# A new order table for a gated linear attention kernel: other turns on every engine, other engines for some operations, 82 fill-in matmuls

## The chip, the cores and the metric

The kernel runs on one core of a Trainium2 chip. The core has five engines that run side by side, each through its own list in order: TensorE (PE, matmuls, with PEld for the weight loads), VectorE (DVE), ScalarE (ACT), GpSimd (POOL) and SyncE (SP, which here only issues DMAs). The metric is the device time of one execution in microseconds (us). The kernel before took 194.0, 195.34 and 195.01 us in three runs, a median of 195.01 us.

## What is computed

Inputs q, k, v, a_re, a_im have the shape (4 batches, 8 heads, 768 steps, 48). Per batch and head a complex state S of 48 x 48 is decayed by a at each step, k v^T is added, and q reads its real part:

```
mag   = sqrt(a_re^2 + a_im^2);  a = (a_re, a_im) * min(mag, 0.999) / (mag + 1e-6)
S_re, S_im = a_re*S_re - a_im*S_im + k v^T,  a_re*S_im + a_im*S_re
y[t]  = q[t] . S_re
x     = y with the heads side by side             # (4, 768, 384)
xn    = (x - mean(x)) / sqrt(var(x) + 1e-6) * g_ln
out   = x + relu(xn @ w_ch1) @ w_ch2              # 384 -> 1536 -> 384
```

## The kernel before

The 768 steps of a batch are cut into six chunks of 128. Two chunks are a pair, so there are twelve pairs (0 to 11), three to a batch, and 24 chunks. Pair P holds chunks 2P and 2P+1. Pair 0 alone does its gate work in two halves of four heads (`.0` and `.1` at the end of a name), so that its first results come earlier.

The recurrence is turned into matmuls. A decay is a magnitude and an angle, and both are summed over the steps of a chunk. For a pair the operations, by the names that the order table uses, are:

- loads on SP: `are`, `aim` (L440), `k`, `q`, `vf` (L399);
- gates: `ln` (L443, ACT) and `iv` (L445, ACT) of a_re, `r` = aim/are, `r2` its square, `u` = ln(1 + r2) (L457, ACT), `l` and `lc`, the log magnitude and its cap (L461, L464, DVE), `th`, the arctan (L480, ACT);
- sums over the steps on PE: `dec` of the log magnitudes (L472) and `ph` of the angles (L487, L491), which takes the last angle of the pair before from `car` (L501 or L504);
- `e` and `en`, exp of plus and minus the sum (L476, ACT), `sin` (L509) and `cos` (L520, or by `abs`, L526 or L528, and L532), with `qt` (L516, PE), which adds a quarter turn for pairs 0 to 3;
- products on DVE or GpSimd (all on line 289, a helper): `ke` = k en, `qe` = q e, and the stacks `ks`, `qs`, each product times cos (`.0`) and times sin (`.1`). `r` and `r2` have the same helper line. `pad` clears the stacks' unused columns;
- the stacks turned round, `ksT`, `qsT`: either by PE (`kT`, `qT`, L588) with a copy by DVE or ACT, or by a transposing DMA from SP (L593);
- `am`, the scores (L611), `atm`, the scores under the causal mask (DVE), `v` in bf16 (L407 or L409), `gm` and `G`, the state carried from chunk to chunk (L635, L639), with the decay from `dps` (L568) and `decc`; `y` (L661, L664), `x` a copy of it;
- the layer norm's sums `bn` (L674, L675) and `rstd` (L698 or L701), and the feed forward: `xtr` and `xT` turn x round (L682), `mm1` is x by w1 in three groups of two parts (L715), `relu` (L726 ACT, L728 DVE), `mm2` by w2 (L736), `ot` the output (L750 on DVE; or `oa` on ACT, L741, and `ot` on GpSimd, L748), `st` its store (L756).

The norm is folded into w1: `wp` and `wc` (L379, L383) change the weights in place, once at the start, after `wl.0` has loaded them (L359, from GpSimd's queue). `wl.1` (L361) loads w2. `tab` (L770) loads ACT's table, one for logarithm and exp, the other for arctan and sine; an ACT operation needs its table to be the one loaded last. `warm` is a fill-in matmul (L765): it multiplies constants into a bank that nobody reads, and needs only the constant `ue`.

What sets the order is one list written out by hand, `PLAN`. A token such as `qs.1.0.0:V` gives an operation, its engine (P, A, V, G, S) and, after P or for an operation that reads PSUM, the bank. `@name` adds a wait for another operation on top of the waits that the data ask for. Each engine runs its tokens in the order of the list, and an operation that must wait holds all that stands behind it on its engine. Operands live in rings of tiles (`RINGS`: three for `q`, two for `vf`, two for `xT` and `h`, and so on), so an operation also waits until the tile's former use is over; and PSUM has eight banks, which are handed from one user to the next in the order of the list.

```
for op in steps:
    if op.behind:
        tc.add_manual_dep(made[op.name][0], made[op.behind][-1].name, info,
                          reason="turns at the shared port")
```

Of the kernel before, what the change touches and what calls it, by code (L numbers as in the profile page):

```python
# [39 lines left out]
ue:G are.1.0:S are.0.0:S are.0.1:S aim.0.0:S pad.ks.1:G warm.0:P0 warm.1:P0 aim.0.1:S warm.2:P0 zdec:G  # L40
pad.qs.1:G warm.3:P0 warm.4:P0 aim.1.0:S pad.ks.0:G warm.5:P0 warm.6:P0 warm.7:P0 one:G cmean:G warm.8:P0
tab.log.0:A ln.1.0:A pad.qs.0:G warm.9:P0 warm.10:P0 aim.2.0:S qrow:G warm.11:P0 ln.0.0:A warm.12:P0 car0.1:G
warm.13:P0 warm.14:P0 iv.0.0:A car0.0:G warm.15:P0 warm.16:P0 pad.qs.2:G k.0.1:S ln.0.1:A warm.17:P0
warm.18:P0 pick:G warm.19:P0 iv.0.1:A r.0.0:V warm.20:P0 q.1.0:S iv.1.0:A warm.21:P0 warm.22:P0 r2.0.0:V
warm.23:P0 r.0.1:V warm.24:P0 u.0.0:A warm.25:P0 q.0.1:S warm.26:P0 r2.0.1:V warm.27:P0 uth:V u.0.1:A
warm.28:P0 r.1.0:V warm.29:P0 gln:S warm.30:P0 warm.31:P0 warm.32:P0 r2.1.0:V warm.33:P0 warm.34:P0 are.2.0:S
warm.35:P0 warm.36:P0 l.0.0:V warm.37:P0 warm.38:P0 tab.trig.1:A th.0.1:A warm.39:P1 lc.0.0:V th.1.0:A
ph.0.1:P0 k.0.0:S dec.0.0:P1 th.0.0:A car.0.1:V0 l.0.1:V sin.0.1:A0 q.0.0:S ph.0.0:P2 warm.40:P3 warm.41:P3
car.0.0:V2 q.1.1:S wgc:V ph.1.0:P4 lc.0.1:V tab.log.2:A u.1.0:A k.1.1:S wl.0:G@lc.0.1 dec.0.1:P3 car.1.0:V4
qt.0.1:P0 ln.2.0:A vf.0.0:S l.1.0:V warm.42:P6 ident:G warm.43:P6 warm.44:P6 warm.45:P6 e.0.0:A1 warm.46:P6  # L50
warm.47:P6 vf.0.1:S iv.2.0:A warm.48:P6 lc.1.0:V dec.1.0:P6 en.0.1:A3 r.2.0:V k.1.0:S en.0.0:A1 e.1.0:A6
are.3.0:S r2.2.0:V e.0.1:A3 qe.1.0.0:V u.2.0:A dps.0:P1 ke.0.0.0:V qe.0.0.0:V warm.49:P3 warm.50:P3 l.2.0:V
warm.51:P3 warm.52:P3 warm.53:P3 warm.54:P3 warm.55:P3 warm.56:P3 qe.0.1.0:V warm.57:P3 warm.58:P3
tab.trig.3:A sin.0.0:A2 ke.0.1.0:V cos.0.1:A0 qt.0.0:P2 lc.2.0:V sin.1.0:A4 warm.59:P3 qs.0.0.1:V warm.60:P3
ks.0.0.1:V cos.0.0:A2 ks.0.1.0:V qt.1.0:P4 qs.0.1.1:V th.2.0:A ks.0.1.1:V dps.1:P0 ks.0.0.0:V cos.1.0:A4
kT.1:P2 decc.1:V0 qs.0.1.0:V kT.0:P0 qs.0.0.0:V ksT.1:V2 qT.0:P3 qe.1.0.1:G@qs.0.0.0 qT.1:P4 qsT.0:V3 mask:G
aim.3.0:S tab.log.4:A en.1.0:A6 wp.0:P5 decc.0:V1 qs.1.0.1:V qsT.1:A4 dec.2.0:P2 qs.1.0.0:V vf.1.1:S wc.0.0:V5
ke.1.0.1:G@qs.1.0.0 ksT.0:A0 am.1:P6 wc.0.1:V5 qT.3:P4 vf.1.0:S ke.1.0.0:G e.2.0:A2 wc.0.2:V5 am.0:P0
en.2.0:A2 v.0:G q.2.1:S qsT.3:V4 ks.1.0.0:V ln.3.0:A gm.0:P2 q.2.0:S ph.2.0:P4 atm.1:V6 ks.1.0.1:G@ks.1.0.0
G.0:A2 iv.3.0:A k.2.0:S gm.1:P2 qT.2:P3 atm.0:V0 y.1:P6 r.3.0:G k.2.1:S kT.3:P7 G.1:V2 wp.1:P0 qsT.2:V3  # L60
tab.trig.5:A sin.2.0:A4 are.4.0:S y.0:P1 kT.2:P2 ksT.3:V7 x.0:A1 v.1:G qt.2.0:P4 th.3.0:A ksT.2:V2 xtr.0:P7
aim.4.0:S wl.1:G gm.2:P1 wc.1.0:V0 x.1:A6 ph.3.0:P2 G.2:A1 wc.1.1:V0 qe.2.0.0:G cos.2.0:A4 xtr.1:P6 wc.1.2:V0
gm.3:P1 xT.0:A7 qe.2.0.1:G am.3:P4 sin.3.0:A2 xT.1:V6 wp.2:P0 atm.3:V4 qs.2.0.0:G car.3.0:A2 am.2:P6 qt.3.0:P2
atm.2:V6 mm1.0.0.0:P4 cos.3.0:A2 qs.2.0.1:G mm1.0.0.1:P4 G.3:V1 y.3:P2 wc.2.2:V0 relu.0.0:A4 y.2:P1 x.3:V2
# [10 lines left out]
ot.1:V2 mm2.3.1:P1 iv.6.0:A bn.2:V mm1.2.0.1:P4 st.0:S bn.4:V rstd.1:G mm1.2.0.0:P4 st.1:S qs.3.0.1:V
mm1.2.1.1:P6 qs.3.0.0:V tab.trig.7:A th.5.0:A mm2.3.2:P1 ks.3.0.1:V relu.2.0:A4 ot.2:V0 mm1.2.1.0:P6 l.5.0:V
st.2:S qT.6:P2 th.4.0:A vf.3.1:S qT.7:P0 q.4.0:S qe.4.0.1:G@l.5.0 qsT.6:A2 kT.7:P3 qsT.7:V0 are.8.0:S
ph.4.0:P4 ke.4.0.0:G ksT.7:V3 relu.2.1:A6 are.7.0:S ot.3:V1 kT.6:P0 sin.4.0:A4 mm1.2.2.0:P2 r.6.0:V abs.4.0:A4
am.7:P6 vf.4.1:S ksT.6:V0 ke.4.0.1:G@r.6.0 mm1.2.2.1:P2 car.4.0:A4 atm.7:V6 cos.4.0:A am.6:P0 k.5.0:S
# [24 lines left out]
relu.5.2:V0 ph.9.0:P4 x.12:A3 y.13:P3 ot.9:V6 sin.9.0:A4 mm2.10.0:P0 qs.7.0.1:V x.13:A3 mm2.11.1:P2 abs.9.0:V4
car.9.0:A4 qsT.15:S xtr.13:P1 xtr.12:P3 ks.7.0.1:V mm2.10.1:P0 xT.12:V3 ksT.15:S mm2.10.2:P0 v.7:V
# [696 lines left out]
```

## Time and profile before

| | |
|---|---|
| three runs, us | 194.0, 195.34, 195.01 |
| span of the profiled execution, us | 193.1 |
| time of the profiled execution beside its span | not given on the page; the median of the runs is 1.9 above the span |
| busy: PE, DVE, ACT, POOL | 91%, 79%, 83%, 54% |
| first `mm1` matmul (L715) starts at, us | 39.79 |
| last matmul ends at about, us | 188.3 |
| granted PE clock | full, but for 24.0 to 27.4 (0.50) and the end |
| DMA | 37.04 MB, 192 GB/s over the span |

A row of the timeline gives the start and the length in us, the engine, the line, the operation, `out<-in` by the program's tile names without buffer numbers, shapes and a count; in brackets stands the engine's idle time before it and what ended it. A group's row gives the busy time, the mean in ns of one, the idle time before. The busy time of PE is modelled: matmuls are pipelined and their lengths overlap. Several operations share one helper line, so products are told apart by their tiles (`r`, written by `r`, `r2` and `u` alike, holds three of them).

### The profile page before, as it was taken

The page shows a single profiled execution, that of the slowest core. Times are in us where ns is not written, and L with a number is a line of the kernel's source. Part 1 is how long each engine was busy: PE and PEld are TensorE (multiplying, and loading weights), DVE is VectorE, ACT ScalarE, POOL GpSimd, SP SyncE. Part 2 cuts the span into 40 slices and gives each one's busy share as a digit, 9 for nine tenths or more (in the row PEclk, how much of TensorE's full clock was granted, in tenths as well). Part 3 has the DMA queues.
Part 4 walks back from the last instruction along what each step waited for, and adds up shares of the span by engine and source line. Part 5 has one row for each costly group of instructions (what it writes and reads, how often), then busy time and mean ns, then how long its engine had stood idle before and what let it go on. Part 6 is the DMA issues. An engine that isn't in the chain of part 4 may idle for free.

```text
span 193.1 us, 5126 instructions
## 1 busy us (share of the span) xinstructions
PE 175.3 (91%) x2042; PEld 133.6 (69%) x2042; DVE 151.7 (79%) x276; ACT 159.4 (83%) x222; POOL 104.8 (54%) x123
## 2 busy tenths in 40 slices
PE   5856597999999999999999989999989897999991
PEld 3643386689876877877867856868658676776860
DVE  0578979999779999799988978997987695657422
ACT  3899989979999999999989898888999856463460
POOL 8403038998334435489595950544857715593110
PEclk9999969999999999999999999999999999999998
DMA  5999999999999699979999997999997999997132
GB/s 159 275 215 185 201 207 239 213 188 220 210 201 214 195 260 231 220 152 226 188 233 168 212 220 106 195 235 205 230 196 150 140 203 147 252 127 203 44 122 83
DMA packets 129992, 37.04 MB, mean 192 GB/s; under 512 B 124976, under 2 KB 129584, under 8 KB 129968
## 3 DMA queue, kind: packets, MB, share of 16 engines
q1 hardware_dynamic: 128016, 34.35, 85.7%
q0 software_dynamic: 1952, 2.36, 7.4%
q8 instruction: 16, 0.26, 0.6%
q14 instruction: 8, 0.07, 0.1%
HBM read 28.31 MB, written 4.72 MB: 171 GB/s over the span
## 4 chain that ended last, share of the span: by engine, by line
PE 52%; DVE 17%; ACT 12%; DMA 7%; SPq 4%; issue 4%; POOL 2%; DVEq 0%; ACTq 0%
PE banks L736 16%; PE banks L715 15%; PE banks L588 5%; PE banks L611 3%; DMA qsT<-qs 3%; DMA aim<-in_a_im_dram 2%; SPq L593 2%; PE banks L491 2%; ACT L770 2%; DVE l L461 2%; DMA k<-in_k_dram 2%; ACT trig L509 2%; ACT th L480 2%; PE banks L661 2%; PE banks L682 2%
## 5 line engine op out<-in xcount | busy, mean ns | idle before, releaser
L736 PE MATMUL banks<-w2b,h 128*128 128x384 bf16 x288 | 54.5, 326 | 0.7 <-ACT trig L509 0.6
L715 PE MATMUL banks<-xT,w1b 128*128 128x256 bf16 x432 | 51.3, 273 | 0.0
L715 PEld LDWEIGHTS <-w1b 128*128 128x128 bf16 x432 | 41.3, 98 | 6.3 <-DVE xT L286 0.4
L736 PEld LDWEIGHTS <-h 128*128 128x128 bf16 x288 | 26.1, 97 | 14.6 <-issue 1.1
L289 DVE TENSOR_TENSOR atm<-banks,mask 128x1024 bf16<-128x1024 f32 x24 | 28.9, 1219 | 7.4 <-PE banks L611 7.2
L726 ACT ACTIVATE h<-banks 128x1024 bf16<-128x1024 f32 x26 | 26.3, 1020 | 5.4 <-PE banks L715 5.2
L289 POOL TENSOR_TENSOR qe<-q,e 128x384 bf16<-128x384 f32 x18 | 16.4, 917 | 22.8 <-DVE qs L289 8.4
L289 POOL TENSOR_TENSOR qs<-qe,trig 128x768 bf16<-128x768 bf16 x12 | 19.6, 1641 | 7.7 <-DVE ks L289 5.5
L770 ACT ACT_TABLE_LOAD x17 | 21.8, 1283 | 1.1 <-PEq L786 0.8
L289 POOL TENSOR_TENSOR ke<-k,en 128x384 bf16<-128x384 f32 x16 | 14.5, 916 | 9.9 <-DVE l L464 5.6
L289 POOL TENSOR_TENSOR ks<-ke,trig 128x768 bf16<-128x768 bf16 x9 | 14.7, 1642 | 7.7 <-DVE ks L289 6.8
L611 PE MATMUL banks<-qsT,ksT 128*128 128x128 bf16 x192 | 14.6, 219 | 1.7 <-DMA qsT<-qs 1.7
L728 DVE TENSOR_SCALAR h<-banks 128x1024 bf16<-128x1024 f32 x10 | 12.1, 1214 | 4.9 <-PE banks L715 4.9
L748 POOL TENSOR_TENSOR ot<-ot,x 128x384 f32<-128x384 f32 x8 | 7.2, 914 | 15.8 <-ACT ot L741 15.8
L611 PEld LDWEIGHTS <-ksT 128*128 128x128 bf16 x192 | 12.0, 97 | 4.0 <-issue 2.6
L491 PE MATMUL banks<-th,u_th 128*128 128x384 f16 (+1 forms) x52 | 11.9, 313 | 2.5 <-ACT th L480 2.5
L750 DVE SCALAR_TENSOR_TENSOR ot<-banks,rstd,x 128x384 f32<-128x384 f32 x16 | 9.8, 612 | 5.4 <-PE banks L736 3.5
L461 DVE SCALAR_TENSOR_TENSOR l<-r,w 128x768 f16<-128x768 f16 (+1 forms) x13 | 12.0, 926 | 2.0 <-ACT r L457 1.8
L674 DVE BATCH_NORM_STATS2 stats<-x 128x6 f32<-128x384 bf16 x24 | 13.1, 546 | 0.0
L289 POOL TENSOR_TENSOR r<-aim,are 128x768 f16<-128x768 f32 x6 | 10.9, 1817 | 4.1 <-ACT are L445 4.1
L443 ACT ACTIVATE w<-are 128x768 f32<-128x768 f32 (+1 forms) x13 | 10.3, 797 | 2.5 <-DMA are<-in_a_re_dram 2.5
L457 ACT ACTIVATE r<-r,one_b 128x768 f16<-128x768 f16 (+1 forms) x13 | 11.5, 887 | 0.7 <-DVE r L289 0.6
(95 smaller groups left out, 372.6 us busy)
## 6 DMA issues: line engine op xcount, KB each, us to landing
k<-in_k_dram SPq DMA_DIRECT2D x24, 192.0 KB, 4.1
q<-in_q_dram SPq DMA_DIRECT2D x24, 192.0 KB, 4.1
vf<-in_v_dram SPq DMA_DIRECT2D x24, 192.0 KB, 4.1
out_dram<-ot SPq DMA_DIRECT2D x24, 192.0 KB, 3.1
are<-in_a_re_dram SPq DMA_DIRECT2D x11, 384.0 KB, 4.5
aim<-in_a_im_dram SPq DMA_DIRECT2D x11, 384.0 KB, 4.9
w1b<-in_moe_w_ch_dram POOLq DMA_DIRECT2D x1, 1152.0 KB, 11.1
w2b<-in_moe_w_ch_dram POOLq DMA_DIRECT2D x1, 1152.0 KB, 12.5
```

Source lines behind the costliest of these rows:

```text
L289: {"DVE": nc.vector, "POOL": nc.gpsimd}[eng(name)].tensor_tensor(**kw)
L443: add(f"ln.{X}", lambda S_=S_: act(out=S_("w"), in_=S_("are"), func=AF.Ln), needs=[f"are.{X}"], uses=[("are", P), ("w", P)])
L457: add(f"u.{X}", lambda S_=S_: act(out=S_("r2"), in_=S_("r2"), func=AF.Ln, bias=one_b), needs=[f"r2.{X}", "one"], uses=[("r2", P)])
L461: nc.vector.scalar_tensor_tensor(out=S_("l"), in0=S_("r2"), scalar=0.5, in1=S_("w"), op0=ALU.mult, op1=ALU.add)
L491: nc.tensor.matmul(heads(ps[:, c]), lhsT=u_th[:, c, j], rhs=step(T("th", P), j), start=False, stop=(j == R - 1), skip_group_check=True)
L611: nc.tensor.matmul(ps[:, h], lhsT=T("ksT", n)[:, h], rhs=T("qsT", n)[:, h], start=True, stop=True)
L674: nc.vector.bn_stats(out=T("stats", n), in_=T("x", n))
L715: nc.tensor.matmul(ps[:, jj], lhsT=w1b[:, dc, ts(gi * JG + jj, C)], rhs=T("xT", P)[:, dc].rearrange("p c t -> p (c t)"), start=(dc == 0), ...
L726: act(out=dst, in_=src, func=AF.Relu)
L728: nc.vector.tensor_scalar(out=dst, in0=src, scalar1=0.0, scalar2=None, op0=ALU.max)
L736: nc.tensor.matmul(bank(f"o.{n}")[:, 0:DM], lhsT=T("h", P)[:, j, ts(c, C)], rhs=w2b[:, j], start=(j == 0), stop=(j == NJ - 1))
L770: g.add(f"tab.{nm}.{i}", lambda tab=tab: nc.scalar.preload_act_table_set(tab))
```

## The change

The order table is replaced as a whole; below it only the number of fill-in operations changes. Against the table before:

- the loads of pair 0's a_re stand ahead of pair 1's, and other loads have other turns: q of pair 0 comes behind a_im of pair 2 and k of pair 1, for example;
- on ACT the second half's `u` of pair 0 stands behind `th` and a change of tables; `sin` and `cos` of pairs 0 and 1 stand in one stretch; on DVE `car.0.0` stands ahead of `l.0.0`;
- 23 manual waits become 40. Most hold a GpSimd operation until a DVE one is over; `wl.0` waits for `ke.0.0.0`, `wl.1` for `gm.2`, and three hold fill-ins (for `u.0.0`, `car.0.0`, `qe.0.1.0`), and with them all fill-ins behind;
- products on GpSimd: `ke` 16 as before, `qe` 18 to 16, `ks` 9 to 6, `qs` 12 to 5. Squares (`r2`) on GpSimd: none before, four now (pairs 3, 6, 8, 9); on DVE 7 to 4, on ACT 6 to 5;
- other single operations change sides: `ot` on GpSimd 8 to 6 (with `oa` on ACT), `r` on GpSimd 6 to 7, `rstd` on ACT 4 to 6, `xT` on ACT 7 to 10, `car` on ACT 5 to 3, `decc` on ACT 3 to 1; the copies `qsT.1` and `ksT.0` go from ACT to DVE, `qsT.3` from DVE to ACT;
- `ksT.18` is turned by PE and copied by DVE instead of by a DMA;
- 61 fill-ins become 82: none is left before the first `u` but two, and there are 20 between `dps.1` and the first `qt`;
- at the end the list is `mm2.22` whole and then `mm2.23`, where it was both in turns.

The core of the diff (the first lines of the two tables, parts in which the stacks of pair 10 and the last chunks are made, and the loop):

```diff
 PLAN = """
-ue:G are.1.0:S are.0.0:S are.0.1:S aim.0.0:S pad.ks.1:G warm.0:P0 warm.1:P0 aim.0.1:S warm.2:P0 zdec:G
...
-warm.13:P0 warm.14:P0 iv.0.0:A car0.0:G warm.15:P0 warm.16:P0 pad.qs.2:G k.0.1:S ln.0.1:A warm.17:P0
-warm.18:P0 pick:G warm.19:P0 iv.0.1:A r.0.0:V warm.20:P0 q.1.0:S iv.1.0:A warm.21:P0 warm.22:P0 r2.0.0:V
...
-dps.10:P2 k.11.0:S ks.10.0.1:V gm.18:P3 k.11.1:S am.19:P6 G.18:A3 vf.10.1:S qe.10.0.0:G@ks.10.0.1 mm2.16.0:P0
...
-oa.21:A2 ot.20:V3 mm1.11.2.1:P0 relu.11.1:A6 bn.22:V ot.21:G mm2.22.0:P2 relu.11.2:A0 mm2.23.0:P4 st.21:S
-st.20:S mm2.22.1:P2 rstd.11:A st.19:S mm2.23.1:P4 mm2.23.2:P4 mm2.22.2:P2 ot.23:V4 ot.22:V2 st.23:S st.22:S
+are.0.1:S ue:G zdec:G uth:V car0.0:G@uth ident:G@uth pick:G@uth one:G qrow:G tab.log.0:A ln.0.1:A iv.0.1:A are.0.0:S
+ln.0.0:A iv.0.0:A are.1.0:S ln.1.0:A mask:G iv.1.0:A aim.0.0:S r.0.0:V r2.0.0:V car0.1:G u.0.0:A aim.0.1:S
+r.0.1:G@r2.0.0 tab.trig.1:A th.0.1:A aim.1.0:S r.1.0:V r2.1.0:V th.1.0:A r2.0.1:V q.1.1:S warm.0:P0 warm.1:P0
+warm.2:P0@u.0.0 warm.3:P0 warm.4:P0 warm.5:P0 warm.6:P0 warm.7:P0 warm.8:P0 warm.9:P0 warm.10:P0 warm.11:P0 warm.12:P0
+warm.13:P0 warm.14:P0 warm.15:P0 warm.16:P0 ph.0.1:P0 th.0.0:A tab.log.2:A u.0.1:A warm.17:P1 warm.18:P1 warm.19:P1
+warm.20:P1 warm.21:P1 ph.0.0:P7 car.0.0:V7 l.0.0:V are.2.0:S lc.0.0:V warm.22:P1 warm.23:P1 warm.24:P1@car.0.0
...
+qs.10.0.1:G@qs.10.0.0 am.19:P0 rstd.8:G mm2.17.1:P6 G.18:A2 gm.19:P2 st.14:S mm2.17.2:P6 y.18:P4 atm.19:V0
...
+st.18:S st.20:S relu.11.1:V6 mm2.22.1:P2 oa.21:A5 bn.22:V rstd.11:A mm2.22.2:P2 st.19:S ot.22:V2 st.22:S mm2.23.0:P4
+ot.21:G st.21:S mm2.23.1:P4 mm2.23.2:P4 ot.23:V4 st.23:S
 """
...
-    for i in range(61):
+    for i in range(82):
         g.add(f"warm.{i}", lambda i=i: nc.tensor.matmul(
```

More of the change, by code (lines that the diff above doesn't have):

```diff
@@ L60 @@
[L60 to L64, printed above, removed]
@@ L75 @@
[L75 to L79, printed above, removed]
```

173 lines of the change are left out of this document (88 added, 85 removed).

## The prediction

> **What bounds the kernel now.** I read the page first: the span, the busy shares and the chain that ended last.
>
> ```profile
> span 193.1 us, 5126 instructions
> PE 175.3 (91%) x2042; PEld 133.6 (69%) x2042; DVE 151.7 (79%) x276; ACT 159.4 (83%) x222; POOL 104.8 (54%) x123
> PE 52%; DVE 17%; ACT 12%; DMA 7%; SPq 4%; issue 4%; POOL 2%; DVEq 0%; ACTq 0%
> ```
>
> PE is busy 91% and carries half of the chain. The share hides two stages, so the second view is busy time by stretches, cut at the first L715 matmul and at the last L736 one (columns: stretch, length, busy us and count on PE, weight loads, DVE, ACT, POOL; granted clock; DMA share; GB/s).
>
> ```profile
> 0.00:39.80 39.80, 30.02 (x318) 22.12 (x319) 29.59 (x61) 34.58 (x50) 19.80 (x42) 0.96 0.98 212
> 39.80:80.00 40.20, 40.20 (x485) 32.06 (x485) 35.67 (x65) 38.70 (x52) 22.11 (x24) 1.00 1.04 216
> 80.00:130.00 50.00, 48.66 (x611) 37.18 (x610) 45.98 (x80) 45.75 (x64) 31.58 (x29) 1.00 0.94 193
> 130.00:165.00 35.00, 32.60 (x371) 24.57 (x368) 27.20 (x52) 28.37 (x37) 20.85 (x19) 1.00 1.04 184
> 165.00:188.30 23.30, 23.30 (x265) 17.54 (x264) 12.07 (x22) 12.02 (x21) 10.45 (x11) 1.00 0.69 147
> 188.30:193.10 4.80, 0.56 (x4) 0.10 (x2) 1.24 (x2) 0.00 (x0) 0.00 (x0) 0.81 0.23 84
> ```
>
> From 39.8 to 188.3 PE idles only 1.34 + 2.40 = 3.7 us of 148.5. So a new order can win in three places: the front (39.8 us, a chain of latencies before the big products start), the 3.7 us in the middle, and the tail (4.8 us). PE's own list from the first L715 on is nearly a constant.
>
> **The change, part by part.** First the front; its rows of the timeline (start, length, engine, line):
>
> ```profile
> 2.22 6.82 PE L765 MATMUL banks<-u_e 128*128 128x256 f16 x40 [2.22 <-POOL u_e L323]
> 7.07 0.56 DVE L289 TENSOR_TENSOR r<-aim,are 128x384 f16<-128x384 f32 x1 [7.07 <-DMA aim<-in_a_im_dram]
> 8.12 0.61 ACT L457 ACTIVATE r<-r,one_b 128x384 f16<-128x384 f16 x1
> 9.55 1.28 ACT L770 ACT_TABLE_LOAD   x1
> 10.46 0.55 DVE L461 SCALAR_TENSOR_TENSOR l<-r,w 128x384 f16<-128x384 f16 x1
> 10.85 1.67 ACT L480 ACTIVATE th<-r 128x384 f16<-128x384 f16 x3
> 13.18 0.36 DVE L504 TENSOR_SCALAR car<-banks 32x192 f16<-32x192 int16 x1
> 39.79 1.48 PE L715 MATMUL banks<-xT,w1b 128*128 128x256 bf16 x12
> ```
>
> *Loads.* DVE's first product waits for `aim.0.0`. Three loads stand ahead of it in both tables, with the same bytes (are.1.0, are.0.0, are.0.1; now are.0.1, are.0.0, are.1.0). So `aim.0.0` lands when it did, the product starts at 7.07, and the first `u` (L457) at 8.12: pair 0's loads first win nothing by themselves.
>
> *The order on ACT and DVE.* The table load for arctan now follows the first `u` at once (8.7 instead of 9.55), so the three `th` end near 11.7 instead of 12.5. But `car.0.0` now stands ahead of `l.0.0` on DVE, and `l.0.0` ran at 10.46: it must now wait for `ph.0.0` on PE, and everything of DVE's front is queued behind it.
>
> *The fill-in matmuls.* All but two now wait for the first `u`; 15 of them stand ahead of `ph.0.1`, five more ahead of `ph.0.0`. Their price is shown by the same matmuls of before in two stretches:
>
> ```profile
> 2.20:6.90 4.70, 4.68 (x23) 3.22 (x23) 1.00 1.08 290
> 7.00:9.00 2.00, 2.00 (x19) 1.57 (x17) 1.00 1.00 267
> ```
>
> The first 23 took 4.70/23 = 0.20 us each, the next 19 took 2.00/19 = 0.105: PE ran at half speed for its first 4.7 us, although no granted clock is listed as low there. Before, that was over by 6.9, with nothing behind it. Now it starts at 8.8: 15 x 0.20 = 3.0 brings us to 11.8, `ph.0.1` costs about 0.5 to 1.0, five more 0.5 to 1.0, `ph.0.0` 0.5 to 1.0 (six matmuls of about 0.08 warm), so `car.0.0` starts between 13.6 and 15.1, against 13.18. The Trainium skill ("TensorE: Matmul & The Clock Gate", "What's actually happening") says that the default state is throttled and that a free-running window of 3.4 us of activity releases it; by it the lower or the upper end comes out as the window happens to lie, and the rows above agree with the half speed.
>
> From `car.0.0` (at T) I add the listed durations along DVE's new list: `l`, `lc` of pair 0, `l.1.0`, `car.0.1`, `lc.1.0`, `wgc` end at T + 4.6, products and `r.2.0` at T + 7.5, the first stack is complete at T + 12.5, the copies and masks of chunks 0 to 3 run to `wc.1.0` at T + 22.4: 36.0 to 37.5, where before had this:
>
> ```profile
> 24.00:27.40 3.40, 3.40 (x33) 3.22 (x31) 2.38 (x7) 2.63 (x4) 1.35 (x3) 0.50 0.89 174
> 28.22 1.02 ACT L284 COPY ksT<-banks 128x1024 bf16<-128x1024 bf16 x1
> 36.06 2.05 DVE L383 SCALAR_TENSOR_TENSOR w1b<-w1b,gln,banks 128x512 bf16<-128x512 bf16 x3
> 41.11 0.19 PE L661 MATMUL banks<-v,atm 128*128 128x48 bf16 x1
> 41.92 0.82 PE L715 MATMUL banks<-xT,w1b 128*128 128x256 bf16 x6
> ```
>
> In this count the stall of 24.0 to 27.4 is already gone: there PE transposed at clock 0.50, and the new fill-ins (18 behind `qe.0.1.0`) keep it busy just ahead, worth half of 3.4 = 1.7; two copies like the 1.02 one also leave ACT (one comes). So the late `l.0.0` eats what these win. The first L715 comes at 39.7 to 41.2 instead of 39.79; middle **+0.65**. By then `y.2` is done, which before ran behind it: `y.3` and `y.2` took 41.92 - 41.11 = 0.81, half is **-0.4**. New transposes (`kT.18`, 8 matmuls instead of a DMA) add 8 x 0.056 = **+0.45**:
>
> ```profile
> 43.72 0.89 PE banks L588 x16
> ```
>
> (0.89/16). The other 21 fill-ins lie in waits of the front.
>
> *Products and squares.* GpSimd's products fall from 55 to 43, and it gains four squares.
>
> ```profile
> L289 POOL TENSOR_TENSOR qs<-qe,trig 128x768 bf16<-128x768 bf16 x12 | 19.6, 1641 | 7.7 <-DVE ks L289 5.5 <-DVE qe L289 1.4 <-DVE l L464 0.5
> L289 DVE TENSOR_TENSOR ks<-ke,trig 128x768 bf16<-128x768 bf16 x13 | 7.4, 570 | 0.1
> L289 DVE TENSOR_TENSOR qs<-qe,trig 128x768 bf16<-128x768 bf16 x10 | 5.3, 543 | 0.0
> L289 DVE TENSOR_TENSOR qe<-q,e 128x384 bf16<-128x384 f32 x6 | 3.3, 549 | 0.0
> L289 POOL TENSOR_TENSOR r<-aim,are 128x768 f16<-128x768 f32 x6 | 10.9, 1817 | 4.1 <-ACT are L445 4.1
> L409 POOL TENSOR_SCALAR v<-vf 128x768 bf16<-128x768 f32 x5 | 4.2, 834 | 1.3 <-DVE l L464 1.3
> ```
>
> DVE gains three `ks` (0.57), seven `qs` (0.54) and two `qe` (0.55): 6.6 us, less a few squares and copies, about +5 in all; ten products of 1.64 and two small ones leave GpSimd. No GpSimd square is in the trace: it lies between one operand (0.83) and two f32 ones (1.82); I take 1.64, the 16-bit row, 6.6 us for four. All of this lies beside PE. The direct cost is 0 as long as DVE stays ahead: in 39.8 to 80 it has 40.2 - 35.67 = 4.5 us free and gets pair 2's four products, 2.2. What may be won is latency: a `qs` that is late is 1.1 us less late.
>
> ```profile
> PE banks L611 <- DMA qsT<-qs: 1.7, 2, 1.1
> PE banks L682 <- DVE x L286: 0.7, 1, 0.7
> PE banks L736 <- ACT trig L509: 0.6, 1, 0.6
> 152.65 1.64 POOL ks L289
> 158.75 4.99 DMA qsT<-qs
> ```
>
> The largest middle wait is for transposing DMAs behind products of pair 10, where GpSimd's `ks` stands in the chain. In the new table three of pair 10's products go to DVE, but `ks.10.0.1` and `qs.10.0.1` come to GpSimd, so I count only part. Elsewhere the score products (`am`) and `y` stand a little further ahead of the L715 that needs them. I take **-1.2** of 3.7, with +4 as the other end.
>
> *Added waits.* 40 manual waits instead of 23, nearly all GpSimd behind DVE. Behind `wl.1` (now behind `gm.2` on PE) stand the square `r2.3.0` and pair 2's products, for which DVE's `ks` and `qs` wait; and w2b itself:
>
> ```profile
> 35.86 1.09 POOL L361 DMA_DIRECT2D w2b<-in_moe_w_ch_dram  x1
> w2b<-in_moe_w_ch_dram POOLq DMA_DIRECT2D x1, 1152.0 KB, 12.5
> 51.03 1.16 PE L736 MATMUL banks<-w2b,h 128*128 128x384 bf16 x6
> ```
>
> Issued at about 38.1 it lands at 50.6, where the first L736 stands: 0 at best, 1 to 2 us if the load is slow; I take 0. On SP `q.5.0` now waits for GpSimd's `qe.2.0.0` (near 43.4) with pair 2's and 3's v, q, k behind it; the burst of w2b covers that.
>
> *The tail.* Two output products ran behind the last matmul:
>
> ```profile
> 188.30 1.27 DVE L750 SCALAR_TENSOR_TENSOR ot<-banks,rstd,x 128x384 f32<-128x384 f32 x2 [3.04 <-PE banks L736]
> ```
>
> Now chunk 22 is finished whole before chunk 23's twelve matmuls, so one stays: **-0.6**.
>
> Sum: +0.65 - 0.4 + 0.45 - 1.2 - 0.6 = -1.1 on the profiled span of 193.1. The page gives no time beside the span; the median 195.0 is 1.9 above it, and I carry that 1.9 along: 192.0 + 1.9 = **193.9**.
>
> **The rivals.**
> 1. *The middle closes* (faster): front at its lower end (-0.05), middle idle down to 1, wins about 0.7 + 1.5 more: 191.7. For it: longer leads and fewer 1.64 us links; against: PE's waits were caused by DMA, DVE and ACT alike.
> 2. *DVE becomes the pace* (slower). DVE has 5 us more to do, most of it wanted by PE two groups later. It decides when DVE waits more than about 2.3 us (4.5 free less 2.2) between 40 and 80, for GpSimd products that now wait for DVE in turn. Price: the 5 us less what is won, about +3: 198. For it: ACT and DVE lie at 96% and 89% there; against: DVE's idle time later (4.0 of 50, 7.8 of 35).
> 3. *The late warm-up* (slower or same): T at 15.1 or later, +0.8 over the forecast, and with it the w2b or load waits of 1 us: 195.7. By the Trainium skill's window it would come out so in half of the runs.
> 4. *It doesn't do what it says*: the counts by engine are as stated, so no chance is kept for it.
>
> **How the numbers follow.** Forecast (192.4 to 195.3) 0.43; rival 1 0.22; rival 2 0.22; rival 3 0.13. One percent (1.95 us, about what a measurement here can tell) puts the line at 193.05 and 196.95: faster 0.22 and a third of the forecast's chance, 0.36; slower 0.22 and a little of rival 3 and the forecast, 0.27; same 0.37. The range takes in rival 1's lower half and rival 2's price: 190.8 to 198.3.
>
> **What would show it.** In the profile after: fill-ins at 0.20 us each up to 11.8 or later; `l.0.0` behind 13.6; no clock of 0.50 near 24; the first L715 at 39.7 to 41.2; PE idle in the middle under 3.7 us; one `ot` behind the last matmul. I am wrong if PE's middle idle exceeds 5 us with DVE or POOL as releaser, or if the front moves by over 2 us.

## The result, and the profile after

The changed kernel takes **193.11 us** (median of 20 runs, 191.52 to 194.63) against 194.12 us for the kernel before, run beside it (20 runs, 193.46 to 195.41): a ratio of **0.994**, 95% interval 0.9915 to 0.9964. The forecast was 193.9. Ratios leave out the runs that lie over 1.5% above the fastest of their kernel; medians and ranges are over all runs. The median hides two groups. Ten runs took 191.52 to 192.50 us at a mean TensorE clock of 0.999 to 1.000, ten took 193.72 to 194.63 us at 0.989 to 0.990; between the two there is no run. The profile is of a run of the lower group (191.71 us, span 190.0), so it shows 3.1 us less than the profile of before and not the 1.0 of the medians. Of the two profiles only that of before has a stretch at half clock in the front. Line numbers in it are four lower than before: L711 is the old L715, L732 the old L736, L285 the old L289, L457 the old L461. In the kernels of the experiments they are shifted by a few lines in the same way.

The page of after: span, busy shares, and the chain that ended last, by engine.

```profile
span 190.0 us, 5180 instructions
PE 173.9 (92%) x2071; PEld 134.4 (71%) x2071; DVE 158.3 (83%) x288; ACT 158.6 (83%) x221; POOL 90.1 (47%) x111
PE 81%; DVE 12%; DMA 3%; issue 1%; SPq 1%; ACT 0%; DVEq 0%; ACTq 0%
```

TensorE now carries 81% of the chain instead of 52%. The stretches of after, cut at the first L711 matmul, the last L732 one and the same inner marks as before (columns: stretch, length, busy us and count on PE, weight loads, DVE, ACT, POOL; granted clock; DMA share; GB/s):

```profile
0.00:41.95 41.95, 30.25 (x354) 22.32 (x355) 30.64 (x59) 35.12 (x52) 22.67 (x44) 1.00 0.97 217
41.95:80.00 38.05, 38.02 (x466) 30.29 (x463) 35.68 (x68) 36.78 (x48) 20.41 (x23) 1.00 1.02 213
80.00:130.00 50.00, 49.89 (x619) 38.95 (x618) 48.26 (x88) 47.89 (x65) 27.48 (x25) 1.00 1.06 210
130.00:165.00 35.00, 35.00 (x430) 27.26 (x428) 30.14 (x55) 30.05 (x41) 17.41 (x19) 1.00 0.91 183
165.00:185.80 20.80, 20.78 (x219) 15.61 (x214) 12.93 (x22) 8.72 (x18) 2.17 (x3) 1.00 0.40 105
185.80:190.00 4.20, 0.00 (x0) 0.00 (x0) 0.62 (x1) 0.00 (x0) 0.00 (x0) 0.94 0.30 109
```

So the time went as follows. The **front** is 2.16 us longer (41.95 instead of 39.79). The **middle**, from the first L711 to the last L732 matmul, is 5.24 us shorter: it ends at 185.78 instead of 188.86, and lasts 143.83 us instead of 149.07. Of this the idle time that the view shows is 3.6 us (3.74 before, 0.03 + 0.11 + 0.00 + 0.02 now); 0.44 is `y.2`, which moved into the front; the rest, about 1.2, lies in stalls too short for a view whose matmul ends are modelled (counted by the gaps between matmul starts, there are roughly 6 us of stalls before and 1 after; the sum depends on what is called a gap). The **tail** is the same, 4.2 us. 2.16 - 5.24 - 0.02 = -3.1.

The front of after in the timeline (start, length, engine, line; the first four rows lead to `car.0.0`, the three of VectorE behind the dots stand on the chain that ended last, and the last three rows are GpSimd's at that time):

```profile
7.63 0.56 DVE L285 TENSOR_TENSOR r<-aim,are 128x384 f16<-128x384 f32 x1 [5.14 <-DMA aim<-in_a_im_dram]
9.36 3.10 PE L761 MATMUL banks<-u_e 128*128 128x256 f16 x15 [6.55 <-ACT r L453]
12.80 0.71 PE L761 MATMUL banks<-u_e 128*128 128x256 f16 x5
14.05 0.36 DVE L500 TENSOR_SCALAR car<-banks 32x192 f16<-32x192 int16 x1 [2.65 <-PE banks L487]
...
20.61 1.30 DVE L285 TENSOR_TENSOR qe<-q,e 128x384 bf16<-128x384 f32 x1
22.89 1.48 DVE L457 SCALAR_TENSOR_TENSOR l<-r,w 128x768 f16<-128x768 f16 x1
24.77 1.00 DVE L285 TENSOR_TENSOR qe<-q,e 128x384 bf16<-128x384 f32 x1
20.56 2.12 POOL L285 TENSOR_TENSOR qe<-q,e 128x384 bf16<-128x384 f32 x2
22.64 0.91 POOL L285 TENSOR_TENSOR ke<-k,en 128x384 bf16<-128x384 f32 x1
24.45 0.91 POOL L285 TENSOR_TENSOR ke<-k,en 128x384 bf16<-128x384 f32 x1 [0.89 <-DVE l L457]
```

The fifteen fill-ins ran at 0.20 us each up to 12.4, as expected, and `car.0.0` came at 14.05, inside the 13.6 to 15.1. New are VectorE's three rows: `qe` takes 1.30 and 1.00 us where its group had 549 ns before, and `l` 1.48 where others of its shape take 0.96 (a row further down). A product of GpSimd's runs beside each.

Two questions follow. What divides the runs into two groups? And what closed the middle, while lengthening three operations of the front?

### The profile page after: what moved, and what is told of

Read it like the earlier page. It is cut to its first block, busy times and chain, and to the rows that moved or that the text cites. A ratio compares the mean times of both kernels' runs of the same rounds, so it can differ in the third digit from the quotient of the medians.

```text
span 190.0 us, 5180 instructions
## 1 busy us (share of the span) xinstructions
PE 173.9 (92%) x2071; PEld 134.4 (71%) x2071; DVE 158.3 (83%) x288; ACT 158.6 (83%) x221; POOL 90.1 (47%) x111
## 4 chain that ended last, share of the span: by engine, by line
PE 81%; DVE 12%; DMA 3%; issue 1%; SPq 1%; ACT 0%; DVEq 0%; ACTq 0%
PE banks L711 24%; PE banks L732 23%; PE banks L607 6%; PE banks L584 6%; PE banks L487 3%; PE banks L468 3%; DMA aim<-in_a_im_dram 3%; PE banks L761 3%; PE banks L657 2%; PE banks L635 2%; PE banks L678 2%; PE banks L660 2%; DVE l L457 2%; PE banks L483 2%; DVE qe L285 2%
## 5 line engine op out<-in xcount | busy, mean ns | idle before, releaser
L732 PE MATMUL banks<-w2b,h 128*128 128x384 bf16 x288 | 53.0, 326 | 0.0
L711 PE MATMUL banks<-xT,w1b 128*128 128x256 bf16 x432 | 52.4, 273 | 0.0
L711 PEld LDWEIGHTS <-w1b 128*128 128x128 bf16 x432 | 40.6, 98 | 5.0 <-DVE xT L282 0.2
L732 PEld LDWEIGHTS <-h 128*128 128x128 bf16 x288 | 26.3, 97 | 14.6 <-ACT h L722 0.2
L285 DVE TENSOR_TENSOR atm<-banks,mask 128x1024 bf16<-128x1024 f32 x24 | 29.3, 1220 | 5.6 <-PE banks L607 4.4
L722 ACT ACTIVATE h<-banks 128x1024 bf16<-128x1024 f32 x26 | 26.2, 1023 | 6.6 <-PE banks L711 3.3
L761 PE MATMUL banks<-u_e 128*128 128x256 f16 x82 | 12.8, 298 | 10.4 <-ACT r L453 6.6
L285 POOL TENSOR_TENSOR ke<-k,en 128x384 bf16<-128x384 f32 x16 | 14.6, 913 | 10.1 <-DVE l L460 5.9
L285 POOL TENSOR_TENSOR r<-aim,are 128x768 f16<-128x768 f32 (+1 forms) x7 | 11.9, 1697 | 14.2 <-ACT h L722 10.1
L285 POOL TENSOR_TENSOR qe<-q,e 128x384 bf16<-128x384 f32 x16 | 14.8, 934 | 7.7 <-ACT rstd L695 3.7
L761 PEld LDWEIGHTS <-u_e 128*128 128x128 f16 x82 | 8.3, 106 | 12.9 <-ACT r L453 7.0
L744 POOL TENSOR_TENSOR ot<-ot,x 128x384 f32<-128x384 f32 x6 | 5.5, 913 | 25.2 <-DVE ot L746 13.4
L285 POOL TENSOR_TENSOR ks<-ke,trig 128x768 bf16<-128x768 bf16 x6 | 9.8, 1640 | 8.7 <-DVE qs L285 5.9
L746 DVE SCALAR_TENSOR_TENSOR ot<-banks,rstd,x 128x384 f32<-128x384 f32 x18 | 10.8, 609 | 2.7 <-PE banks L732 2.7
L457 DVE SCALAR_TENSOR_TENSOR l<-r,w 128x768 f16<-128x768 f16 (+1 forms) x13 | 12.1, 929 | 0.1
L285 POOL TENSOR_TENSOR qs<-qe,trig 128x768 bf16<-128x768 bf16 x5 | 8.2, 1641 | 8.2 <-DVE qs L285 2.9
```

The costliest lines, as they stand in the source:

```text
L285: {"DVE": nc.vector, "POOL": nc.gpsimd}[eng(name)].tensor_tensor(**kw)
L457: nc.vector.scalar_tensor_tensor(out=S_("l"), in0=S_("r2"), scalar=0.5, in1=S_("w"), op0=ALU.mult, op1=ALU.add)
L711: nc.tensor.matmul(ps[:, jj], lhsT=w1b[:, dc, ts(gi * JG + jj, C)], rhs=T("xT", P)[:, dc].rearrange("p c t -> p (c t)"), start=(dc == 0), ...
L722: act(out=dst, in_=src, func=AF.Relu)
L732: nc.tensor.matmul(bank(f"o.{n}")[:, 0:DM], lhsT=T("h", P)[:, j, ts(c, C)], rhs=w2b[:, j], start=(j == 0), stop=(j == NJ - 1))
L746: nc.vector.scalar_tensor_tensor(out=T("ot", n), in0=bank(f"o.{n}")[:, 0:DM], scalar=T("rstd", P)[:, ds(c, 1)], in1=T("x", n), op0=ALU.mul ...
```

## The experiments: the clock

**Fill-ins in the kernel before.** Eighteen fill-in matmuls ahead of the half-speed stretch of 24.0 to 27.4 us, with the old order (a name in the table, and the engine after the colon; P is TensorE):

```
 warm.58:P3
+warm.61:P3 ... warm.70:P3
 ...
 warm.60:P3
+warm.71:P3 ... warm.74:P3
 ...
 dps.1:P0
+warm.75:P3 ... warm.78:P3
```

> The kernel before with 18 more fill-ins between 20 and 24 us (10 behind the ten that stand there, 4 behind the next two, 4 behind dps.1). Theory (the stretch at clock 0.50 comes from PE's idle time ahead of it and costs half of 3.4 us): the stretch goes, 16 transposes of pair 0 take 0.9 instead of 1.7, the first L715 comes 1 to 1.5 us earlier, time down by about 1.2. Rival (DVE's list paces the front): the stretch goes, and the time moves by less than 0.4.

Measured: 192.57 us median (191.98 to 193.76, 12 runs), ratio 0.9917 [0.9892, 0.9942]; the first `mm1` matmul (L710 there) came at 38.69 instead of 39.79. Eighteen matmuls whose results nobody reads give the old order more than the new order gives in its median, 1.6 us against 1.0.

**The changed kernel without its fill-ins 48 to 67**, which stand between `dps.1` and the first `qt`:

```
-warm.48:P4 warm.49:P4 warm.50:P4@qe.0.1.0 warm.51:P4 ... warm.67:P4
```

> The changed kernel without the 20 fill-in matmuls 48 to 67 between dps.1 and the first qt. Theory (they are what keeps TensorE's clock at full behind 24 us): clock 0.50 over 3.41 us somewhere from 23 to 30 us in all runs or nearly all, mean clock 0.99 or less, one group of times at 193.5 to 194.8 us. Rival (the other work there is enough, or the stall is hidden): two groups as with them, median 193.0 to 193.3 us.

Measured: 194.06 us median (193.22 to 194.84, 10 runs), ratio 0.9997 [0.9967, 1.0028], and the clock 0.973 to 0.981 in all ten. One group, as the theory said. The stretches of its profile, cut at the steps of its clock:

```profile
19.73:23.15 3.42, 1.03 (x37) 0.80 (x36) 3.31 (x7) 3.39 (x5) 3.42 (x5) 1.00 1.10 185
23.15:29.97 6.82, 5.20 (x28) 3.03 (x28) 6.16 (x15) 5.41 (x9) 2.01 (x3) 0.50 1.09 223
29.97:33.39 3.42, 3.42 (x53) 3.01 (x51) 2.69 (x5) 3.40 (x5) 3.42 (x4) 1.00 0.67 136
```

After 3.42 us in which TensorE was busy for 1.03, the clock is 0.50 for 6.82 us, twice 3.41. The first `mm1` matmul (L709) comes at 43.49 instead of 41.95, 1.5 us later, of which 0.3 is a later `car.0.0` (14.33). The prediction gave this part of the change 1.7. The median is 2.0 us above that of the lower group (192.09).

**Fourteen more fill-ins** in the two waits that are left, behind `warm.49` and behind `qt.1.0`:

```
 warm.49:P4
+warm.82:P4 ... warm.89:P4
 ...
 qt.1.0:P2
+warm.90:P1 ... warm.95:P1
```

> The changed kernel with 14 more fill-in matmuls: eight in TensorE's wait of 20.9 to 22.0 us and six in its wait of 25.7 to 26.9 us, nothing else changed. Theory (the upper half of the changed kernel's runs, 193.7 to 194.6 us at a mean clock of 0.989 to 0.990, are those in which one window of 3.41 us falls back to clock 0.50 behind these two waits; 3.41/2 = 1.7 us): all runs near 191.5 to 192.5, mean clock 0.995 or more in each, median about 192.0. Rival (the upper group comes from a late release of the clock at the start, 9 to 14 us): both groups stay, median 193.0 to 193.3.

Measured: 192.09 us median (191.25 to 193.34, 6 runs), ratio 0.9901 [0.9862, 0.9939], the clock 0.994 or more in all six; no run above 193.4. So the upper group had a window at half clock in this place, by the clocks: no run of that group was profiled, but the profile of a kernel with the same list on TensorE (the first in the section on the front, clock 0.987) has it from 26.20 to 29.61 us. What spread remains has another cause, and the profile happens to be of the slowest of the six (193.34 us): its clock is released only at 15.37 us, and `car.0.0` comes at 15.67, beyond the 15.1 at which the third rival began.

This also says what the order itself is worth when both kernels have fill-ins against the window: 192.09 us here against 192.57 for the old order with its eighteen, 0.5 us, with ranges that overlap (four of those twelve runs still show a mean clock of 0.986 to 0.988).

**Thirty fill-ins at the very start**, behind the constant `ue` that they multiply, beside the table as it is:

```
 ue:G
+warm.0:P0 warm.1:P0 warm.82:P0 ... warm.111:P0
 ...
-warm.0:P0 warm.1:P0
```

> The changed kernel with 30 more fill-ins right behind ue, so that PE is busy from 2.2 us on as before, and nothing else changed. Theory (the changed kernel's runs fall into two groups, near 192.0 and 194.2, because its PE is released from half speed at a time that varies from run to run): PE is at full speed before 9 us, the 15 fill-ins ahead of ph.0.1 take 0.11 us each, the upper group disappears, runs lie within 1.2 us, median about 191.3. Rival (the two groups come from the loads or from something later): still two groups 2 us apart, median within 0.5 of 193.1.

Measured: **191.33 us** median (191.04 to 191.77, 6 runs), ratio 0.9855 [0.9821, 0.989]: the best of all kernels here, 1.45% under the kernel before. Its timeline:

```profile
2.22 5.11 PE L764 MATMUL banks<-u_e 128*128 128x256 f16 x32 [2.22 <-POOL u_e L322]
8.86 1.81 PE L764 MATMUL banks<-u_e 128*128 128x256 f16 x15 [1.53 <-ACT r L456]
```

The fifteen that took 3.10 us take 1.81 here, since the slow time is spent while nothing waits for it. `car.0.0` comes at 12.45, 1.6 us sooner, of which 0.5 is an earlier load. But a half-clock window comes back in this profile:

```profile
22.29:25.71 3.42, 2.42 (x18) 1.28 (x17) 3.34 (x11) 2.77 (x5) 0.00 (x0) 1.00 1.09 209
25.71:29.12 3.41, 3.41 (x34) 3.41 (x33) 2.20 (x7) 3.38 (x5) 1.98 (x2) 0.50 1.04 218
```

**Both sets of fill-ins** were to take that away.

> Both sets of fill-ins at once: the 30 early ones behind the constant they multiply, and the 14 in the two waits near 20 and 24.5 us. Its profile without the 14 showed clock 0.50 from 25.7 to 29.1 us. Theory (that stretch delays the transposes by about 1.5 us and TensorE is what everything waits for from there on): 189.8 to 190.6 us, first L714 matmul about 1 us earlier than with the early ones alone. Rival (behind 26 us VectorE and ScalarE set the pace, so the slow stretch is hidden there): 191.0 to 191.8 us, as with the early ones alone, at a clock of 1.00.

Measured: 192.29 us median (191.99 to 192.50, 4 runs), ratio 0.9901 [0.9865, 0.9937]. The clock stayed full in its profile and the time is no better: 1 us worse than with the early ones alone. The rival was nearer, and still too low. The middle lasts 144.87 us there instead of 143.82. In the runs with the early ones alone the clock did not matter either: 191.06, 191.77 and 191.31 us at 0.991, 191.47 and 191.35 at 1.000 (and 191.04 at 0.996). So the window accounts for the upper group of the changed kernel, but with `car.0.0` 1.6 us sooner it costs nothing that these runs show. Why that is so, and why the additional fill-ins cost time, was not settled.

## The experiments: products and order

**The new order on the old engines**, and **the old order on the new engines**. Twenty `ks` and `qs` products changed sides; each kernel has them moved back or moved alone, at their places in its own table (V is VectorE, G is GpSimd). Three manual waits of moved products in each of the two tables go with them.

```
-ks.2.0.1:V
+ks.2.0.1:G
...
-qs.10.0.1:G@qs.10.0.0
+qs.10.0.1:V
```

> The changed kernel with its new order, but the 20 ks and qs products that changed sides run on the engine that they had before (10 more of them on GpSimd in all). Theory A (moving products to VectorE is what closed the middle): TensorE's idle time between the first L711 and the last L732 matmul back to 2.5 us or more with products or their transposing DMAs as releaser, time 195 to 197 us. Theory B (the order closed it, the scores and the moe chunks standing further ahead): idle time under 0.8 us, time 192.3 to 193.8 us.

> The kernel before with its own order, but the 20 ks and qs products on the engines that the changed kernel gives them. Theory A (moving products to VectorE closes the middle): TensorE's idle time between the first L715 and the last L736 matmul falls from 3.7 to under 1.5 us, time 191.5 to 192.8 us. Theory B (the order closes it): idle time 3 us or more, time 193.8 to 196 us.

Measured: the new order on the old engines 210.41 us (208.49 to 210.72, 4 runs), ratio 1.0809; the old order on the new engines 198.37 us (197.63 to 198.83, 4 runs), ratio 1.0207 [1.0166, 1.0247]. Both theories said that one half of the change carries the gain, and both fell by their times: **each half alone is a loss**. By TensorE's waits in the middle the new order on the old engines did what theory A said (8.2 us, 5.8 of them for GpSimd's own `qs` and `ks`), and the old order on the new engines what theory B said (5.1 us idle, where 3 or more was forecast). How the gain is shared out between them can't be told. Neither is a clean half, either: fifteen products come to GpSimd in the first kernel and five in the second, all without a manual wait, so a half with waits fitted to it was not tried. The page of the first tells more:

```profile
span 206.7 us, 5189 instructions
PE 178.4 (86%) x2071; PEld 135.8 (66%) x2071; DVE 168.2 (81%) x278; ACT 158.7 (77%) x221; POOL 112.2 (54%) x121
```

VectorE has ten instructions fewer than after (278, not 288) and is busy 9.9 us longer. So its instructions themselves got longer.

**The new order without the manual waits of the middle.** A name behind the @ is a manual wait: GpSimd's `r.5.0` waits for `r.4.0`, and so on. Order and engines stay as they are, and 23 such waits go.

```
-r.5.0:G@r.4.0
+r.5.0:G
-qe.3.0.1:G@lc.4.0
+qe.3.0.1:G
...
```

> The changed kernel with the same order and the same engines, without the 23 manual waits of GpSimd that stand behind wl.1 in the table (from r.5.0 on). Theory (what the waits do is to put GpSimd's products beside VectorE's work on PSUM instead of beside its products and its l, which take 1.4 to 2.2 us instead of 0.55 to 0.95 when a GpSimd product runs beside them): VectorE busy 163 us or more instead of 158.3, TensorE's idle time in the middle over 1 us, time 195 to 200 us. Rival (the order alone keeps them apart, the waits are spare): VectorE busy within 1 us of 158.3, time 192.3 to 193.8 us.

Measured: 203.85 us (203.49 to 206.91, 4 runs), ratio 1.05 [1.0452, 1.0549], beyond even the 200 us of the theory. The page, with the same 288 instructions on VectorE, then the same groups of VectorE instructions in both kernels (columns: count, busy us, mean ns), first without the waits, then after:

```profile
PE 177.1 (88%) x2069; PEld 135.6 (67%) x2071; DVE 171.1 (85%) x288; ACT 159.0 (79%) x221; POOL 94.1 (47%) x111
```

```profile
L284 DVE TENSOR_TENSOR atm<-banks,mask 128x1024 bf16<-128x1024 f32 x24 | 29.2, 1218 | 6.4 <-PE banks L606 5.5 <-ACT v L402 1.0
L456 DVE SCALAR_TENSOR_TENSOR l<-r,w 128x768 f16<-128x768 f16 x11 | 12.8, 1166 | 0.0
L284 DVE TENSOR_TENSOR ks<-ke,trig 128x768 bf16<-128x768 bf16 x16 | 11.7, 765 | 0.2
L284 DVE TENSOR_TENSOR qs<-qe,trig 128x768 bf16<-128x768 bf16 x17 | 10.9, 659 | 0.2
L284 DVE TENSOR_TENSOR qe<-q,e 128x384 bf16<-128x384 f32 x8 | 7.5, 934 | 0.0
```

```profile
L285 DVE TENSOR_TENSOR atm<-banks,mask 128x1024 bf16<-128x1024 f32 x24 | 29.3, 1220 | 5.6 <-PE banks L607 4.4 <-ACT v L403 1.0 <-ACT are L441 0.3
L457 DVE SCALAR_TENSOR_TENSOR l<-r,w 128x768 f16<-128x768 f16 x11 | 11.0, 997 | 0.0
L285 DVE TENSOR_TENSOR qs<-qe,trig 128x768 bf16<-128x768 bf16 x17 | 9.1, 552 | 0.5 <-POOL qe L285 0.3
L285 DVE TENSOR_TENSOR ks<-ke,trig 128x768 bf16<-128x768 bf16 x16 | 8.3, 552 | 0.2
L285 DVE TENSOR_TENSOR qe<-q,e 128x384 bf16<-128x384 f32 x8 | 5.6, 700 | 0.0
```

The products and `l` got longer by 2 to 3 us a group, and `atm`, which reads PSUM, did not. TensorE pays for it: in the middle the list of its waits is empty for after, and has 9.5 us here, every one for VectorE. The longest (line, what it waited for, us in all, times, longest):

```profile
PE banks L710 <- DVE dec L281: 1.9, 1, 1.9
PE banks L563 <- DVE xT L281: 1.8, 1, 1.8
PE banks L656 <- DVE atm L284: 1.8, 1, 1.8
```

A half-clock stretch from 100.53 to 103.94 us can account for at most 1.7 us more. One place of the timeline without the waits shows how a product gets longer:

```profile
77.10 0.55 DVE L284 TENSOR_TENSOR qs<-qe,trig 128x768 bf16<-128x768 bf16 x1
77.23 1.92 POOL L284 TENSOR_TENSOR qs<-qe,trig 128x768 bf16<-128x768 bf16 x1
77.57 2.00 DVE L284 TENSOR_TENSOR ks<-ke,trig 128x768 bf16<-128x768 bf16 x1
```

A product of the same shape takes 0.55 us when it starts just ahead of GpSimd's, and 2.00 us when it starts behind it. I counted over this profile which VectorE instructions run beside GpSimd's products of over 0.8 us for more than 0.6 of their own shortest time (the shortest of the same tile, operation and shape in any profile here). Of 23 that read SBUF alone (`ks`, `qs`, `ke`, `qe`, `l`, `r`, `v`), 18 were stretched by more than 0.06 us; of 78 others (sources in PSUM, or batch-norm statistics) none. Which of the two starts first decides it: all 18 started while a GpSimd product ran, and ended a fixed time after its end (0.41 to 0.43 us for `ks`, `qs`, `ke` and `qe`, 0.81 for the 128x768 `l`), as if they worked only then; the other 5 started 0.05 to 0.38 us before it. Over all VectorE instructions that read SBUF alone the stretching is 15.8 us here, 16.4 with the new order on the old engines, 4.4 with the old order on the new engines, 2.1 in the changed kernel and 1.5 in the one before. The Trainium skill ("GPSIMD Engine Reference", "8. Key points") says that GpSimd shares its SBUF interfaces with VectorE and contends with instructions in a 2-port mode or with two SBUF inputs. The trace agrees, and puts a number to it that the page does not give: up to 1.5 us on an instruction of 0.55.

So this is what the waits do for the new order: they lay GpSimd's work beside VectorE's work on PSUM. After has ten `ks` and `qs` products more on VectorE than before, and behind 26 us one stretched instruction, by 0.1 us (`ke` at 145.20). This shows what the middle would lose without the waits, and not what closed it: the old order kept the two engines apart as well, with three stretched instructions behind 26 us, 1.4 us in all. Which part of the new table took away TensorE's waits of before stays open.

## The experiments: the front

**Other turns for GpSimd's products of pair 1**, since three of them lie beside `qe.0.1.0`, `l.2.0` and `qe.0.0.0`:

```
-qe.1.0.0:G@r.2.0   qe.1.0.1:G@ke.0.1.0   ke.1.0.1:G@qe.0.1.0   ke.1.0.0:G@l.2.0
+qe.1.0.0:G@qe.0.1.0   qe.1.0.1:G@qe.0.1.0   ke.1.0.1:G@l.2.0   ke.1.0.0:G@qe.0.0.0
```

> The changed kernel with other manual waits for four GpSimd products of pair 1: both qe behind DVE's qe.0.1.0, ke.1.0.1 behind l.2.0, ke.1.0.0 behind qe.0.0.0. Theory (DVE's qe.0.1.0 at 1.30 us and l.2.0 at 1.48 us are stretched by GpSimd products that run at the same time): these fall to about 0.55 and 0.96, the first L715 comes 1 us earlier, both groups of runs move down by about 1, median near 192.1. Rival (DVE has that time to spare, or GpSimd's products come too late): 0 or slower by up to 1.

Measured: 194.47 us (191.64 to 195.90, 12 runs), ratio 0.997 [0.9931, 1.0009]: no gain. Its timeline says why:

```profile
20.49 0.55 DVE L285 TENSOR_TENSOR qe<-q,e 128x384 bf16<-128x384 f32 x1
22.02 1.70 DVE L457 SCALAR_TENSOR_TENSOR l<-r,w 128x768 f16<-128x768 f16 x1
24.12 1.00 DVE L285 TENSOR_TENSOR qe<-q,e 128x384 bf16<-128x384 f32 x1
25.05 1.33 DVE L285 TENSOR_TENSOR ks<-ke,trig 128x384 bf16<-128x384 bf16 x2
```

The first `qe` is back at 0.55, and the stretch went to `l` (1.70) and to `ks`, 1.9 us in all instead of 1.7. The half-clock window is also there in 11 of the 12 runs, by their clocks; their median is 194.47, against 194.17 for the upper group of after, so at the same clock there is no gain either.

**`l.0.0` and `lc.0.0` ahead of `car.0.0`**, alone and then with the thirty early fill-ins:

```
 ph.0.0:P7
+l.0.0:V lc.0.0:V
 ...
 car.0.0:V7
-l.0.0:V
...
-lc.0.0:V
```

> The changed kernel with l.0.0 and lc.0.0 ahead of car.0.0 on DVE. Theory (the front's DVE list starts late because it is queued behind car.0.0, which waits for PE): l.0.0 runs at 11.4, everything of DVE behind car.0.0 comes 0.85 us earlier, time down by 0.6 to 0.8. Rival (from there ACT's order, the second u behind two table loads, paces the front): less than 0.3.

> The 30 early fill-ins and l.0.0 and lc.0.0 ahead of car.0.0 together. The two profiles of the single edits: car.0.0 at 12.45 us with the early ones (14.05 without), and l.1.0 1.17 us behind the start of car.0.0 with l first (1.92 us without). Theory (both lie on the one chain that sets the front, VectorE's list up to the first stack): 190.3 to 191.0 us. Rival (behind 25 us TensorE's own list or the loads set the pace, as with the further fill-ins, which brought the clock to 1.00 and no time): 191.0 to 191.8 us.

Measured: alone 193.19 us (192.42 to 194.97, 12 runs), ratio 0.9963 [0.9936, 0.999], the median of after. But the mix is another: eleven of the twelve runs have a clock of 0.989 to 0.991, and their median of 193.19 is 1.0 us under the upper group of after (194.17), which is what the theory said and a little more. The one run at full clock, 192.42 us, is no better than the lower group. With the early fill-ins it was 191.62 us (191.12 to 193.61, 6 runs), ratio 0.989 [0.9845, 0.9935], the same as the early ones alone. VectorE's rows in the second:

```profile
12.50 0.36 DVE L503 TENSOR_SCALAR car<-banks 32x192 f16<-32x192 int16 x1 [0.79 <-PE banks L490]
13.79 0.56 DVE L460 SCALAR_TENSOR_TENSOR l<-r,w 128x384 f16<-128x384 f16 x1 [0.93 <-ACT r L456]
14.38 0.26 DVE L463 TENSOR_SCALAR l<-l 128x384 f16<-128x384 f16 x1
14.62 0.96 DVE L460 SCALAR_TENSOR_TENSOR l<-r,w 128x768 f16<-128x768 f16 x1
```

The next `l` waits for ScalarE until 13.79 here, and with the early ones alone it starts at 13.74, behind `l.0.0`. So beside the early fill-ins the late `l.0.0` is free: it fills that wait. In the changed kernel as it is, `car.0.0` comes later than that and the late `l.0.0` does cost: `l.1.0` starts 1.92 us behind `car.0.0`, and 1.17 with `l.0.0` first.

**GpSimd's two `ke` of pair 1 behind `l.2.0` and its products**, with the early fill-ins:

```
-ke.1.0.1:G@qe.0.1.0   ke.1.0.0:G@l.2.0
+ke.1.0.1:G@qs.1.0.0   ke.1.0.0:G@qs.1.0.0
```

> The 30 early fill-ins, and GpSimd's products ke.1.0.1 and ke.1.0.0 wait for VectorE's qs.1.0.0 instead of qe.0.1.0 and l.2.0, so that neither runs beside l.2.0. Theory (l.2.0 takes 1.47 us instead of 0.95 because ke.1.0.1 runs beside it, and it stands on the front's chain): l.2.0 at 0.95 us, dec.2.0 about 0.5 us sooner behind it, first L714 matmul near 40.8 us instead of 41.3, time 190.6 to 191.1 us. Rival (the product does not stretch it, or ks.1.0.1 comes late in its place and takes the gain back): l.2.0 as it was or kT.3 later than 32.5 us, time 191.1 to 191.8 us.

Measured: 191.59 us (191.11 to 192.63, 6 runs), ratio 0.9857 [0.9814, 0.9899], no different from the early fill-ins alone. VectorE's rows of its timeline at this place:

```profile
21.84 0.96 DVE L460 SCALAR_TENSOR_TENSOR l<-r,w 128x768 f16<-128x768 f16 x1
23.21 0.56 DVE L288 TENSOR_TENSOR qe<-q,e 128x384 bf16<-128x384 f32 x1
```

`l` is at 0.96 again (1.47 with the early ones alone), so the product beside it was what stretched it. But `ks.1.0.1` ends at 32.31 instead of 31.37, `kT.3` starts at 32.83 instead of 32.53, and the first L714 matmul at 41.60 instead of 41.30: the rival was right that what GpSimd does later comes late.

## Why the prediction was right, and where it was not

The sign of the median's change and its size (-1.1 forecast, -1.0 measured) agree, and the agreement of the size is luck. In the profile the front came out 1.5 us longer than forecast, the middle 4.1 shorter (-5.24 against -0.4 + 0.45 - 1.2) and the tail 0.6 longer, together -3.1 instead of -1.1; half of the runs then lie 2.1 us higher, by a window at half clock that the forecast had counted as gone.

- **The front, +0.65 forecast, +2.16 measured,** over the 2 us that the prediction itself named as a sign of being wrong. `car.0.0` at 14.05 lies in its range, but 0.56 us of it is a load: the first product started at 7.63 and not at 7.07, so "`aim.0.0` lands when it did" did not hold in this run. The step that failed is "from `car.0.0` (at T) I add the listed durations along DVE's new list": `wc.1.0` came at T + 24.0 and not at T + 22.4. The three stretched instructions take 0.75 + 0.53 + 0.45 = 1.73 us more than the listed durations, which were taken as fixed although the list put GpSimd products beside them. They are not the whole of it: the `ks` products of pair 0 were done at T + 13.3, only 0.8 behind the T + 12.5 given for the first stack, so the count had some 0.9 us to spare up to there. From there to `wc.1.0` VectorE took 10.7 us, without a wait or a stretched row, where the count has 9.9.
- **"So the late `l.0.0` eats what these win."** In part, as the kernel stands: about 0.75 us of the front, by the start of `l.1.0`. With the early fill-ins it costs nothing, since it lies in a wait for ScalarE.
- **The fill-ins at half speed, 0.20 us each up to 11.8 or later,** and the stall of 24.0 to 27.4 gone: both held in the profile. The 1.7 us for the second is 1.5 by the first `mm1` matmul of the kernel without those fill-ins, 0.3 of it from a later `car.0.0`. What the forecast missed is that the stall is gone only in half of the runs, by their clocks.
- **The middle: -0.4, +0.45 and -1.2 forecast, -5.24 measured.** The step that failed is "so I count only part". Every wait of TensorE's middle went, for DMA, VectorE and ScalarE alike, so rival 1 (idle down to 1 us) was right on the middle. That it would cost VectorE nothing directly also held: it is busy 6.6 us more, and TensorE does not wait for it. The prediction's reason, longer leads and fewer slow links, was not tested by itself. What the runs show is a condition it left out: without the waits that keep GpSimd's and VectorE's SBUF work apart, the new order takes over 10 us longer. Rival 1's time is no hit, though the profiled run took 191.71 us: it had the front at its lower end.
- **w2b: 0 forecast, 0 measured.** Issued at 40.16, it landed 9.9 us later at 50.1; the first L732 matmul ran at 52.34.
- **GpSimd's square: 1.64 taken, 1.47 measured,** inside the bounds and off the path.
- **The tail, -0.6 forecast, 0 measured.** The row of two `ot` was misread: the first of the two started at 188.30, and the last matmul ended at 188.86 and not at the 188.3 of the table of before, so only one stood behind it already.
- **Rival 2, VectorE as the pace, 198 us.** It did not happen, and its price was not tested: the products moved without the order give 198.4 us, but with the old waits, and of TensorE's 4.9 us of waits in the middle there 2.6 are for VectorE, the others for DMA, ScalarE and GpSimd.
- **Rival 3, the late warm-up.** It exists: T was 15.67 in one profile of the kernel with fourteen more fill-ins. The rule of the Trainium skill that was cited for it ("TensorE: Matmul & The Clock Gate", "What's actually happening"), a free-running window of 3.4 us, is borne out by the runs as to its length: in the trace's clock record every half-clock stretch between the first release and the last matmul lasted 3.41 us or twice that, and the one of the front began anywhere from 22.9 to 26.2 us. The prediction asked only where that window lies at the start. It also lies somewhere near 26 us, and that is where the two groups of runs part.

## What to carry to other kernels

A duration from a trace holds for the neighbours that the instruction had: where a reordering puts GpSimd elementwise work beside VectorE instructions that read SBUF alone, ask for it again, and lay GpSimd beside VectorE's PSUM work. Spend TensorE's slow start on work that nothing waits for, from the first microsecond on. Where runs fall into groups, put the mean clock beside each time before the medians are compared; and an order table, its engine choices and its waits are tried together, as one without the others cost 2 to 8% here.

## What was not expected of the hardware

- VectorE instructions that read SBUF alone took up to 2.0 us instead of 0.55 beside a GpSimd product, and one with a single source did too (`v<-vf`, 1.61 us, where its shortest is 0.54). Those that read PSUM did not move: `atm` 1218 ns against 1220.
- The half-clock window is not tied to one level of activity. It came after 1.03 us of TensorE work in 3.42, and after 2.42 of 3.42 with the early fill-ins, but the changed kernel kept its full clock after this window with 2.22:

```profile
25.69:29.10 3.41, 2.22 (x33) 1.98 (x33) 3.41 (x12) 3.33 (x4) 0.00 (x0) 1.00 1.09 235
```

  What level and which window count stays open.
